# K and V caches of a decode step loaded through GpSimd's DMA queue, one packet for each DMA engine, instead of SP's

## The chip, the cores and the metric

The kernel runs on one core of one Trainium2 chip. The metric is the device time of one execution in microseconds, from the runs' times; the time before is the median of three. One further execution was recorded by the hardware profiler, and all rows come from it.

## The reference, cut to what matters

One decode step (one new token for each of two sequences) through a layer with attention and MLP in parallel, in float32:

```python
B, Sq, D = 2, 1, 1024;  Hq, Hkv, Sk, Dh = 32, 4, 32768, 128;  F = 3584
xn = _layernorm(x)
# attention over a cache, 8 query heads on each K/V head
q = (xn @ wq).reshape(B, 1, Hq, Dh)
scores = einsum(q, repeat(k_cache, 8)) * Dh ** -0.5
o = einsum(softmax(scores), repeat(v_cache, 8)) @ wo
# MLP
h = silu(xn @ w1)
return x + o + h @ w2
```

K and V are 134 MB each, the four weights 63 MB together. Every byte is read once, and there is little arithmetic on it.

## The kernel before, in words

There are three large buffers in SBUF, `bufA`, `bufB` and `bufC`, each of 128 partitions x 16384 float32 (64 KiB a partition, 8.39 MB). Everything that comes from HBM passes through them. The host has laid out every tensor so that a transfer is 128 rows, each row one contiguous run.

The order of the work is written out by hand, with semaphores between the engines, in three stages:

- **Weights at the head.** `blocks` (L152) lists four blocks of weights: `wq[0]` in `bufA`, `wq[1]` in `bufB`, the first 16384 columns of `w1` in `bufC`, and the remaining 12288 columns of `w1` (the `w1` tail, 6.29 MB) again in `bufB`. `first(u)` waits for the landing of block u and multiplies it with the normalised input; its last matmul's mark on TensorE's semaphore is `last_of[u]`. `second(u)` transposes the result. The first three blocks are loaded as soon as the program runs (`wq[1]` and `w1` after the 8 KB `x`, which ScalarE's queue loads, has landed, L115). The `w1` tail may be loaded once TensorE has read `wq[1]` out of `bufB`, that is after `last_of[1]` (L209).
- **Eight turns of attention.** There are 8 pairs of a K/V head and a sequence (`LOOPS`), and each turn takes four transfers of 8.39 MB: two halves of K into `bufA` and `bufB`, then two halves of V into the same two. `tick(it, k)` is TensorE's mark in turn `it`: 0 and 1 when it has read the K halves, 4 and 5 when it has read the V halves. A transfer into a buffer waits for the mark of the previous reader of that buffer. So there are at most two transfers on their way, one in each buffer. For the first turn the marks are `free = {0: last_of[0], 1: last_of[3]}`: `bufA` is free when `wq[0]` has been read, `bufB` when the `w1` tail has been read. TensorE runs the turns in a hardware loop (L291) and takes each landing off the semaphores `ldA` and `ldB` with `take` (a wait, then a decrement). Between the K and the V halves VectorE and ScalarE do the softmax.
- **Weights at the end.** `wo[0]` into `bufA` after `tick(7, 4)`, `wo[1]` into `bufC`, and `w2` in pieces into `bufB` after `tick(7, 5)` and into `bufA` after `wo[0]` has been read.

All large transfers, of weights and of K and V, are issued by SP through `load` (L204 to L207): wait for the mark, then issue. SP does this strictly in the order of the program text:

```python
    load(bufB[:, :(N1 - 4) * SUB], w1[:, W:], ldB, last_of[1])     # L209
    ...
    free = {0: last_of[0], 1: last_of[3]}
    for it in range(LOOPS):                                          # L231
        load(bufA, kt[b, h, 0], ldA, tick(it - 1, 4) if it else free[0])
        load(bufB, kt[b, h, 1], ldB, tick(it - 1, 5) if it else free[1])
        load(bufA, v[b, h, 0], ldA, tick(it, 0))
        load(bufB, v[b, h, 1], ldB, tick(it, 1))
```

GpSimd fills some constants at the head (L104 to L110) and has no work after that.

Of the kernel before, what the change touches and what calls it, by code (L numbers as in the profile page):

```python
# [18 lines left out]
LOOPS = HKV * B  # L19
# [35 lines left out]
def gqa_plus_mlp_kernel(nc, x, kt, v, wq, wo, w1, w2, out):  # L55


    pe, dve, act, pool = (Stream(nc, e, n) for e, n in
                          ((nc.tensor, "pe"), (nc.vector, "dve"), (nc.scalar, "act"), (nc.gpsimd, "pool")))
    sp = nc.sync  # L60
    sems = [pe.sem, dve.sem, act.sem, pool.sem]

    def sem(name):
        sems.append(nc.alloc_semaphore(name))
        return sems[-1]

    def sb(name, *shape):
        return nc.alloc_sbuf_tensor(name, shape, F32).ap()
# [3 lines left out]

    bufA, bufB, bufC = (sb(n, P, W) for n in ("bufA", "bufB", "bufC"))
    ldA, ldB, ldC, ldx, ldr, done = (sem(n) for n in ("ldA", "ldB", "ldC", "ldx", "ldr", "done"))
    tq, tps, trm, tgd, te, tls, tob = (sem(n) for n in ("tq", "tps", "trm", "tgd", "te", "tls", "tob"))
    ident, ones, sel, fold = sb("ident", P, P), sb("ones", P, P), sb("sel", P, 32), sb("fold", P, 64)
    st = sb("st", P, 2 * NC, 16, 32)
# [18 lines left out]
    def mm(o, lhsT, rhs, start=True, stop=True):  # L96
        return nc.tensor.matmul(o, lhsT, rhs, start=start, stop=stop)  # L97
# [5 lines left out]
    g = nc.gpsimd  # L103
# [100 lines left out]
    def load(buf, src, s, *ticks):  # L204
        for of, n in ticks:
            sp.wait_ge(of.sem, n)
        sp.dma_start(buf, src).then_inc(s, 16)  # L207
# [18 lines left out]
    def tick(it, k):  # L226
        return pe, start + PER * it + k + 1

    dve.eng.sem_inc(tps, NC)
    free = {0: last_of[0], 1: last_of[3]}  # L230
    for it in range(LOOPS):  # L231
        h, b = divmod(it, B)
        load(bufA, kt[b, h, 0], ldA, tick(it - 1, 4) if it else free[0])
        load(bufB, kt[b, h, 1], ldB, tick(it - 1, 5) if it else free[1])
        load(bufA, v[b, h, 0], ldA, tick(it, 0))
        load(bufB, v[b, h, 1], ldB, tick(it, 1))

    def queries(it):
        if it:
# [6 lines left out]
    for it in range(LOOPS):  # L246
        h, b = divmod(it, B)
# [43 lines left out]
    with nc.tensor.While(lambda: nc.tensor.snap(turn) < LOOPS):  # L291
        pe.take(tq)
        for a in range(4):
            buf = (bufA, bufB)[a // 2]
            if a % 2 == 0:
                pe.take((ldA, ldB)[a // 2], 16)
                pe.take(tps)
            for r in range(4):
                for q4 in range(4):
                    n = (4 * (a % 2) + q4) * 4 + r  # L300
                    m = mm(ps[a][32 * q4:32 * q4 + 32, :], qT[:, 32 * r:32 * r + 32], buf[:, n * 512:(n + 1) * 512],
                           r == 0, r == 3)
            if a % 2:
                pe.mark(m, LOOPS)
        pe.take(trm)
        pe.mark(mm(smA[:REP, :P], rm, ident), LOOPS)
        pe.take(tgd)
        pe.mark(mm(smB[:, :REP], ones[:REP, :], gd), LOOPS)
        for a in range(4):
            buf = (bufA, bufB)[a // 2]  # L310
            if a % 2 == 0:
                pe.take((ldA, ldB)[a // 2], 16)
                pe.take(te)
            for j in range(16):
                q4, n = j % 4, 16 * (a % 2) + j
                m = mm(po[32 * q4:32 * q4 + 32, :], st[:, a, j, :], buf[:, n * 512:(n + 1) * 512],
                       a == 0 and j < 4, a == 3 and j >= 12)
            if a % 2:
                pe.mark(m, LOOPS)
        pe.take(tls)  # L320
        pe.mark(mm(smA[:, :REP], ones, lsum), LOOPS)
        pe.take(tob)
        for r in range(4):
            m = mm(smB[:, :REP], ob[:, r * P:(r + 1) * P], sel[:, REP * r:REP * (r + 1)], r == 0, r == 3)
        pe.mark(m, LOOPS)
        nc.tensor.reg_add(turn, turn, 1)
# [6 lines left out]
    def stream(buf, src, cuts, *ticks):  # L333

        for lo, hi in zip(cuts, cuts[1:]):
            s = sem(f"piece{len(pieces)}")
            load(buf[:, lo:hi], src[:, lo:hi], s, *ticks)
            pieces.append((hi, s))
            yield hi, s

    lo = 11 * D
    plan = [
        (bufA, [*stream(bufA, wo[0], (0, W), tick(LOOPS - 1, 4))], 0),
        (bufC, [*stream(bufC, wo[1], (0, W))], 16),
        (bufB, [*stream(bufB, w2[:, :W], (0, 4 * D, W), tick(LOOPS - 1, 5))], 32),
    ]
    acc2 = ps[0]
# [35 lines left out]
    for (hi, landed), (bank, a, e) in zip(ends[4:], banks):  # L383
        pe.wait((landed, 16))
        for j in range(4):
            at = lo + 4 * a + j * (e - a)
            m = mm(bank[32 * j:32 * j + 32, :e - a], hT[:, FT - 1, :], bufA[:, at:at + e - a], False, True)
        act.wait(pe.mark(m))
        i_ot = act.mark(nc.scalar.copy(ot[:, a:e], bank[:, :e - a]))  # L389
    sp.wait_ge(act.sem, i_ot[1])  # L390
    sp.dma_start(out, ot[::8, :]).then_inc(done, 16)
    sp.wait_ge(done, 16)
# [33 lines left out]
```

## Time and profile before

| | |
|---|---|
| time, median of 3 runs | 773.39 us (773.29 to 773.48) |
| span of the profiled execution, first to last instruction | 772.1 us |
| what lies around the span (median less span) | 1.3 us |
| bytes read from HBM | 331.37 MB, 429 GB/s over the span |
| TensorE busy | 389.2 us, 50% of the span |
| VectorE / ScalarE / GpSimd busy | 120.7 / 27.4 / 3.0 us |
| SP's DMA queue (q1) | 99.4% of the 16 DMA engines' span |

In the rows, PE is TensorE, DVE VectorE, ACT ScalarE, POOL GpSimd and SP SyncE; SPq and ACTq are the queues on which those engines issue transfers. A row of a timeline has the start in us from the span's start, the duration in us, engine, line, operation, output<-input, the number of instructions, and in brackets the idle time before them with what ended it. An issue's own duration is only the issuing; "us to landing" in the list of DMA issues is from the issue to the landing. One matmul of the program text appears as two MATMUL records. The profiled execution has no run time of its own beside its span.

### The profile page before, as it was taken

To read this page: it belongs to the slowest core of one execution; us is meant where nothing else is said; L and a number is where in the kernel's file an instruction comes from. 1 tells how busy PE (TensorE), PEld (TensorE's weight loads), DVE (VectorE), ACT (ScalarE), POOL (GpSimd) and SP (SyncE) were. 2 spreads that over 40 slices of the span, in tenths; PEclk is the share of its full clock that TensorE was granted. 3 is DMA by queue.
4 is the path that set the end of the run, shared out by engine and by line. 5 is a ranking of instruction groups with operands and counts; after the bars stand their busy time and mean duration, and the time that the engine had idled before them with its cause. 6 is when DMAs were issued, how large, how long until landed. Compare 5 with 4: busy or idle time off the path is not lost. (4 is left out here: it accounts for less than half of the span.)

```text
span 772.1 us, 5932 instructions
## 1 busy us (share of the span) xinstructions
PE 389.2 (50%) x2752; PEld 124.1 (16%) x2752; DVE 120.7 (16%) x153; ACT 27.4 (4%) x34; POOL 3.0 (0%) x10
## 2 busy tenths in 40 slices
PE   1555554464555454544464545454544464545456
PEld 1111211121111111111121111111111121111112
DVE  2000013111311131113111311131113111311000
ACT  0000101000100000001000100000001000000000
POOL 1000000000000000000000000000000000000000
PEclk9966767767767767767767767767767767767778
DMA  9999999999999999999999999999999999999997
GB/s 384 435 432 435 435 435 435 435 435 435 435 435 432 431 431 435 435 435 435 431 435 435 435 431 435 435 435 435 435 435 435 435 435 435 435 435 435 409 435 317
DMA packets 6676, 331.51 MB, mean 429 GB/s; under 512 B 758, under 2 KB 902, under 8 KB 1292
## 3 DMA queue, kind: packets, MB, share of 16 engines
q1 hardware_dynamic: 6656, 331.37, 99.4%
q8 instruction: 7, 0.11, 0.1%
q10 hardware_dynamic: 12, 0.02, 0.0%
q14 instruction: 1, 0.01, 0.0%
HBM read 331.37 MB, written 0.02 MB: 429 GB/s over the span
## 5 line engine op out<-in xcount | busy, mean ns | idle before, releaser
L97 PE MATMUL po<-bufB,st 128*32 128x512 f32 x512 | 72.3, 728 | 81.9 <-PEq L52 81.9
L97 PE MATMUL ps<-bufB,qT 128*32 128x512 f32 x512 | 71.8, 724 | 82.4 <-PEq L52 82.4
L97 PE MATMUL ps<-bufA,qT 128*32 128x512 f32 x512 | 72.5, 730 | 51.3 <-PEq L52 51.3
L97 PE MATMUL po<-bufA,st 128*32 128x512 f32 x512 | 72.9, 733 | 40.5 <-PEq L52 40.5
L275 DVE TENSOR_REDUCE ls<-st 128x8 f32<-128x1024 f32 x16 | 31.7, 1984 | 231.5 <-PE po L97 231.5
L250 DVE STREAM_TRANSPOSE st<-ps 128x1024 f32<-128x1024 f32 x16 | 20.0, 1249 | 247.8 <-PE ps L97 247.8
L97 PEld LDWEIGHTS po<-bufB,st 128*32 128x32 f32 x512 | 20.0, 131 | 134.2 <-issue 134.2
L97 PEld LDWEIGHTS ps<-bufB,qT 128*32 128x32 f32 x512 | 19.8, 130 | 134.4 <-issue 134.4
L97 PEld LDWEIGHTS ps<-bufA,qT 128*32 128x32 f32 x512 | 20.1, 131 | 97.2 <-issue 97.2
L97 PEld LDWEIGHTS po<-bufA,st 128*32 128x32 f32 x512 | 19.9, 131 | 87.0 <-issue 87.0
L252 DVE TENSOR_REDUCE mx<-st 128x8 f32<-128x1024 f32 x16 | 31.7, 1980 | 0.6
L272 ACT ACTIVATE st<-st 128x1024 f32<-128x1024 f32 x16 | 16.9, 1056 | 356.7 <-DVE st L271 356.1
L97 PE MATMUL ps<-bufB,xnT 128*32 128x512 f32 x112 | 19.0, 763 | 14.1 <-PEq L52 14.1
L271 DVE TENSOR_TENSOR st<-st,gmax 128x1024 f32<-128x1024 f32 x16 | 18.9, 1221 | 0.3
L97 PE MATMUL smA<-ident,rm 128*8 128x128 f32 x16 | 3.4, 301 | 29.4 <-PEq L52 29.4
L97 PE MATMUL ps<-bufC,oT 128*32 128x512 f32 x64 | 9.6, 770 | 10.3 <-DMA bufC<-in_wo 10.3
L97 PE MATMUL ps<-bufC,xnT 128*32 128x512 f32 x64 | 9.8, 783 | 9.6 <-DMA bufC<-in_w 9.6
L97 PE MATMUL smA<-lsum,ones 128*128 128x8 f32 x16 | 3.5, 290 | 19.2 <-PEq L52 19.2
L280 ACT COPY ob<-po 128x512 f32<-128x512 f32 x8 | 4.7, 585 | 238.6 <-PE po L97 238.6
L97 PE MATMUL ps<-bufB,hT 128*32 128x512 f32 x64 | 8.6, 688 | 8.1 <-DMA bufB<-in_w 8.1
L97 PE MATMUL ps<-bufA,oT 128*32 128x512 f32 x64 | 9.1, 729 | 7.1 <-DMA bufA<-in_wo 7.1
L97 PE MATMUL smA<-ident,st 2*128 2x2 f32 x16 | 3.6, 349 | 16.5 <-DVE st L136 16.5
(70 smaller groups left out, 109.7 us busy)
## 6 DMA issues: line engine op xcount, KB each, us to landing
bufB<-in_w SPq DMA_DIRECT2D x2, 6144.0 KB, 37.2
bufA<-in_w SPq DMA_DIRECT2D x1, 3072.0 KB, 36.9
bufB<-in_w SPq DMA_DIRECT2D x1, 2048.0 KB, 34.9
bufA<-in_w SPq DMA_DIRECT2D x1, 1536.0 KB, 40.3
bufA<-in_w SPq DMA_DIRECT2D x2, 512.0 KB, 41.5
bufA<-in_w SPq DMA_DIRECT2D x1, 384.0 KB, 42.3
bufA<-in_kt SPq DMA_DIRECT2D x8, 29.3
bufB<-in_kt SPq DMA_DIRECT2D x8, 29.3
```

The costliest lines, as they stand in the source:

```text
L97: return nc.tensor.matmul(o, lhsT, rhs, start=start, stop=stop)
L250: t = dve.mark(V.transpose(st[:, 2 * c:2 * c + 2].rearrange("p a j m -> p (a j m)"), pair[c]))
L252: m = V.tensor_reduce(mx[:, c, :], st[:, 2 * c:2 * c + 2].rearrange("p a j (r m) -> p m (a j r)", r=4), AX.X, ALU.max)
L271: act.wait(dve.mark(V.tensor_sub(e8[c], e8[c], gmax.to_broadcast([P, 128, REP]))))
L272: nc.scalar.activation(e8[c], e8[c], AF.Exp, scale=SCALE).then_inc(te, 1)
L275: m = V.tensor_reduce(ls[:, c, :], e8[c].rearrange("p n m -> p m n"), AX.X, ALU.add)
L280: nc.scalar.copy(ob, po).then_inc(tob, 1)
```

## The change

The 32 transfers of K and V are issued by GpSimd, with the same waits, the same order and the same shape. Each is asked for as one packet for each DMA engine: 128 rows over 16 engines are eight descriptors (rows of 64 KiB) for each. They count on two new semaphores, `kvA` and `kvB`. SP waits for these in order and hands each landing on by adding 1 to `inA` or `inB`, which TensorE takes in place of `ldA` and `ldB`. When all K and V have landed, GpSimd resets the state of those two semaphores and marks its own; SP waits for that mark at the very end. The weights stay on SP: its program is now the four transfers at the head, the 31 hand-ons, `wo[0]` and `wo[1]`, the last hand-on, then `w2` and the output.

```diff
+    kvA, kvB, inA, inB = (sem(n) for n in ("kvA", "kvB", "inA", "inB"))
...
     free = {0: last_of[0], 1: last_of[3]}
+    landed = 0
+
+    def packed(buf, src, s, *ticks):
+
+        pool.wait(*ticks)
+        g.dma_start(buf, src, single_packet=True).then_inc(s, 16)
+
+    def passed_on(upto):
+
+        nonlocal landed
+        while landed < upto:
+            s, to = ((kvA, inA), (kvB, inB))[landed % 2]
+            sp.wait_ge(s, 16 * (landed // 2 + 1))
+            sp.sem_inc(to, 1)
+            landed += 1
+
     for it in range(LOOPS):
         h, b = divmod(it, B)
-        load(bufA, kt[b, h, 0], ldA, tick(it - 1, 4) if it else free[0])
-        load(bufB, kt[b, h, 1], ldB, tick(it - 1, 5) if it else free[1])
-        load(bufA, v[b, h, 0], ldA, tick(it, 0))
-        load(bufB, v[b, h, 1], ldB, tick(it, 1))
+        packed(bufA, kt[b, h, 0], kvA, tick(it - 1, 4) if it else free[0])
+        packed(bufB, kt[b, h, 1], kvB, tick(it - 1, 5) if it else free[1])
+        packed(bufA, v[b, h, 0], kvA, tick(it, 0))
+        packed(bufB, v[b, h, 1], kvB, tick(it, 1))
+    for s in (kvA, kvB):
+        g.wait_ge(s, 16 * 2 * LOOPS)
+    g.dma_reset(range(kvA.num, kvB.num + 1))
+    g.sem_inc(pool.sem, 1)
+    pool.n += 1
+    passed_on(4 * LOOPS - 1)
...
-                pe.take((ldA, ldB)[a // 2], 16)
+                pe.take((inA, inB)[a // 2])
...
         (bufC, [*stream(bufC, wo[1], (0, W))], 16),
+    ]
+    passed_on(4 * LOOPS)
+    plan += [
         (bufB, [*stream(bufB, w2[:, :W], (0, 4 * D, W), tick(LOOPS - 1, 5))], 32),
     ]
...
+    sp.wait_ge(pool.sem, pool.n)
     sp.wait_ge(act.sem, i_ot[1])
     sp.dma_start(out, ot[::8, :]).then_inc(done, 16)
```

More of the change, by code (lines that the diff above doesn't have):

```diff
@@ L311, in gqa_plus_mlp_kernel @@
             if a % 2 == 0:
-                pe.take((ldA, ldB)[a // 2], 16)
+                pe.take((inA, inB)[a // 2])
                 pe.take(te)
```

## The prediction

> **What bounds the kernel now.** I read the page's 40 slices first, then its DMA queues, then SP's waits, and then SP's and TensorE's timelines around the two places where K/V transfers meet weight transfers.
>
> ```profile
> span 772.1 us, 5932 instructions
> DMA  9999999999999999999999999999999999999997
> GB/s 384 435 432 435 435 435 435 435 435 435 435 435 432 431 431 435 435 435 435 431 435 435 435 431 435 435 435 435 435 435 435 435 435 435 435 435 435 409 435 317
> q1 hardware_dynamic: 6656, 331.37, 99.4%
> q8 instruction: 7, 0.11, 0.1%
> SPq L207 <- PE ps L97: 394.2, 19, 38.3
> ```
>
> The DMA engines are busy from end to end, at 431 to 435 GB/s in all slices but the first, the last and one near the end. The last row is SP's own wait list: SP is idle most of the time, waiting until TensorE has read a buffer. So neither issuing nor computing is the limit: the bytes are, and the time changes only by what changes the rate or leaves the DMA engines with nothing to do. The span is 772.1 us, the median of the runs 773.39: 1.3 us lie around the span, and I carry them over.
>
> The steady state, in SP's timeline (start, duration, ...) and the list of issues (last number: us from issue to landing):
>
> ```profile
> 106.61 0.33 SPq L207 DMA_DIRECT2D bufA<-in_v  x1
> 144.76 0.33 SPq L207 DMA_DIRECT2D bufA<-in_kt  x1
> 667.11 0.33 SPq L207 DMA_DIRECT2D bufB<-in_v  x1
> 687.02 0.33 SPq L207 DMA_DIRECT2D bufA<-in_wo  x1
> bufA<-in_kt SPq DMA_DIRECT2D x8, 29.3
> bufB<-in_v SPq DMA_DIRECT2D x8, 29.3
> ```
>
> From 144.76 to 687.02 lie 28 transfers: 542.26 / 28 = 19.37 us each, for 8.389 MB: 433 GB/s. Issue to landing is 29.3 us, so each transfer is issued 29.3 - 19.37 = 9.9 us before the DMA engines get to it. That cover of 9.9 us is what the change draws on.
>
> **The change, part by part.**
>
> *1. The issue moves to GpSimd.* In the steady state a GpSimd issue may be later than SP's by anything up to 9.9 us at no cost. GpSimd has nothing else to do after the head, and its queue holds the same waits in the same order as SP's did. The trace has no issue by GpSimd. For SP's very first issue, onto idle DMA engines:
>
> ```profile
> 0.73 0.38 SPq L100 DMA_DIRECT2D bufA<-in_wq  x1
> 1.83 0.95 POOL L110 MEMSET oT<- 128x1024 f32 x1
> ```
>
> The first slice moves 384 GB/s and not 435: over 772.1 / 40 = 19.3 us that is 2.26 us lost, of which 0.73 precede the issue. So 1.53 us pass between an issue by SP and full speed. For GpSimd I add 0.7 us of work on the descriptors: bounded below by 0 (it is as quick as SP) and above by some 2 us (two of its longest operations here, the 0.95 us MEMSET). I take a value nearer to the MEMSET than to 0, because I expect GpSimd to write descriptors by program. Total 2.2 us, 1.5 to 3.5. The Trainium skill, "DMA: Bandwidth & Descriptors", section "Latency and other measured facts", gives 1 us to the first byte for GpSimd's path and 0.6 us for SP's; by these 0.4 us stand in place of my 0.7, and the sum below would be 0.3 us less. No run here shows it yet.
>
> *2. One packet instead of eight.* What this can bring is bounded by the rate: 8.389 MB at the best slice's 435 GB/s is 19.28 us against 19.37; 0.08 us x 31 = 2.6 us at most. On the other side, a gap between one GpSimd transfer and the next would cost 31 times its size. I take 0 for both: the slices at 431 and 435 lie within 1% and look alike at any place, so there is hardly a per-packet cost to take away.
>
> *3. SP hands on.* One wait and one increment for each landing, some tenths of a us (SP's whole issue takes 0.33). It lies between landing and matmul, so it comes off the same 9.9 us: 0. `wo[0]` stands behind the 31st hand-on, `w2` behind the 32nd; both landings precede the marks that those loads wait for anyway: 0. The reset at GpSimd's end runs beside the last 60 us of weights: 0.
>
> *4. The first K transfer leaves its place in SP's queue.* This is the part that counts. SP, ScalarE's queue, TensorE and VectorE at the head:
>
> ```profile
> 12.76 0.33 SPq L116 DMA_DIRECT2D bufB<-in_wq  x1
> 13.13 0.44 SPq L117 DMA_DIRECT2D bufC<-in_w  x1
> 51.92 0.33 SPq L207 DMA_DIRECT2D bufB<-in_w  x1
> 52.29 0.44 SPq L207 DMA_DIRECT2D bufA<-in_kt  x1
> 86.59 0.33 SPq L207 DMA_DIRECT2D bufB<-in_kt  x1
> ...
> 3.60 0.54 ACTq L112 DMA_DIRECT2D st<-in_x  x1
> ...
> 22.87 9.15 PE L97 MATMUL ps<-bufA,xnT 128*32 128x512 f32 x64 [2.82 <-PEq L52]
> 42.08 9.78 PE L97 MATMUL ps<-bufB,xnT 128*32 128x512 f32 x64 [10.06 <-PEq L52]
> 62.47 9.83 PE L97 MATMUL ps<-bufC,xnT 128*32 128x512 f32 x64 [9.62 <-DMA bufC<-in_w]
> 77.33 9.22 PE L97 MATMUL ps<-bufB,xnT 128*32 128x512 f32 x48 [4.05 <-PEq L52]
> 96.85 9.70 PE L97 MATMUL ps<-bufA,qT 128*32 128x512 f32 x64 [8.42 <-PEq L52]
> ...
> 89.86 0.17 DVE L242 COPY qT<-qall 128x32 f32<-128x32 f32 x1
> ```
>
> `bufA` is free when `wq[0]` has been read, at 22.87 + 9.15 = 32.02. But SP issues the first K half at 52.29 only, because the `w1` tail stands ahead of it in the queue and waits for `last_of[1]` (42.08 + 9.78 = 51.86). So the DMA engines get `wq[1]`, `w1`, `w1` tail, first K half. That order does a service: the tail lands at 77.3, TensorE reads it until 86.55, SP issues the second K half into the same `bufB` at 86.59, and all that time the first K half (19.4 us, landed at 96.85) keeps the DMA engines busy.
>
> In the changed kernel GpSimd waits for `last_of[0]` alone and issues the first K half at about 32. Then two queues have work. How they share is seen in `x`: 8 KB on ScalarE's queue, issued at 3.60 into the middle of `wq[0]`, had landed when SP, which waits for it, went on at 12.76, while `wq[0]` was still being moved (TensorE starts on it at 22.87). So the DMA engines take turns between queues, after a piece and not after a whole transfer. The Trainium skill says the same (same page, section "Queues, rings and completion order"): each DMA engine goes round the queues and changes only at the end of a packet. By that rule the first K half, one packet for each engine, is moved in one go once its turn comes; by turns of single rows it would share half and half with the weights. The sum is the same under both: by about 81 it is done, before the tail gets its share.
>
> So the order becomes: `wq[1]`'s first part, first K half, rest of `wq[1]`, `w1`, `w1` tail. The bytes up to that point are those of before, so they end where they ended, at about 96.8, but now the `w1` tail is the last of them (`wq[1]` lands some 19.4 us later, at 61.4; TensorE has read it at 71.2, so the tail is still queued well before `w1` ends at 81.8). At 96.8 the DMA engines have nothing: the second K half waits for the tail to be read, the first V half for the first K half, and TensorE turns to that only after the four blocks. From the tail's landing:
> - TensorE reads the tail: from 77.33 to SP's issue at 86.59, 9.26 us; 0.1 us for the landing's signal;
> - GpSimd's issue to full speed: 2.2 us.
>
> The sum is 11.6 us in which nothing moves. It isn't made up later, since the bytes are the limit. What is late next: TensorE starts on the first K half 3.6 us after the tail (89.86 + 0.17 less 86.55, the transposes, SiLU and `qT`), needs 9.7 us, and the first V half is issued some 13.3 us after the tail was read, while the second K half still has 19.4 - (13.3 - 2.2) = 8 us to go: covered, and the steady state goes on as before.
>
> *5. The end.* `wo[0]` is issued at 687.02 when the last V half has about 9.4 us to go. If that is one packet, nothing changes. If it shares row by row, it lands 9.4 us later, and `w2` is issued that much later; but `wo[0]` and `wo[1]`, 2 x 19.3 us, are queued behind: 0.
>
> Forecast: 773.4 + 11.6 = 785.0 us. Its own bounds: 773.4 + 9.4 + 1.5 - 2.6 = 781.7 below, 773.4 + 9.4 + 3.5 = 786.3 above.
>
> **The rivals.**
>
> *A. No hole: the K half doesn't get past the weights.* If the DMA engines serve SP's queue first while it has work, or if the first GpSimd issue comes late enough to be moved beside the tail, the first K half covers the tail's reading as now. Then only part 2 remains: 773.4, or down to 770.8 if one packet brings the full 2.6 us. Against it: `x` got through beside `wq[0]` within 9 us, and 30 us lie between the mark at 32 and the tail's turn. For it: `x` went through ScalarE's queue and not GpSimd's. 10%: 5% faster by over 0.2% (1.5 us, about what a measurement of this kernel can tell from no change), 5% within it.
>
> *B. The hole, and a gap at each transfer.* If the next GpSimd transfer's descriptors are not taken up while the last one is running, each of 31 transfers pays part of a cold start. At a quarter of the 1.53 us: 0.4 x 31 = 12 us, 797; at the whole of it, 47 us, 832. Against it: descriptors can lie ready 9 us ahead. For it: no GpSimd transfer is in the trace. 15% for gaps up to 0.4 us, 5% for more. The Trainium skill (same page, "Measured") has 425 GB/s for large transfers issued by GpSimd; taken as the steady rate, a transfer would be 19.74 us by an estimate from that page, and the time some 11 us above my forecast, inside this case.
>
> *C. Instruction fetches.* The 7 packets of q8 are fetches of code. Beside rows they wait for a row of about 2.4 us (19.37 / 8), beside one packet for up to 19.4 us. Only a fetch that an engine needs at once costs this, and TensorE idles before nearly every block; one exposed fetch would give up to 785 + 9.5 (19.4 less the cover), 795. 3%.
>
> **How the numbers follow.** The forecast has 67%, A 10%, B 20%, C 3%. The range takes in the forecast's own bounds, B's small gaps and C, and leaves out A and the large gaps (15%): 781.0 to 797.0. Faster 0.05, within 0.2% 0.05, slower 0.90.
>
> **What would show it.** In the profile after: an issue of the first K half by GpSimd at about 32; TensorE's start on `wq[1]` at about 61 and not 42; the `w1` tail's matmuls near 97; one slice about 97 to 108 with the DMA share halved, and all later marks 11 to 12 us later; the spacing of transfers still 19.3 to 19.4 us. If TensorE starts on `wq[1]` at 42 and no slice drops, A was right. If the spacing is 19.6 or more, B.

## The result, and the profile after

The changed kernel takes 787.47 us (median of 4 runs, 787.16 to 787.75) against 773.40: 1.0182 times as long, 95% interval 1.0167 to 1.0196. The profiled execution has a span of 786.4 us, 14.3 more. First the page of the changed kernel: the span, the DMA share and the rate in 40 slices, and the two queues.

```profile
span 786.4 us, 5967 instructions
DMA  9999759999999999999999999999999999999997
GB/s 407 447 424 427 324 213 431 457 437 430 427 430 430 427 430 460 433 427 430 430 430 427 453 440 430 427 430 433 427 427 460 433 430 427 430 433 427 428 437 311
q0 software_dynamic: 4608, 268.44, 78.9%
q1 hardware_dynamic: 2048, 62.93, 18.7%
```

The loss has one place: slices 5 and 6, from 78.6 to 118 us, where the DMA share falls to 7 and 5 tenths. Everywhere else the digits are those of before. GpSimd's and SP's issues there (first two fences: start, duration, and the idle time before with what ended it), and TensorE's work:

```profile
32.29 0.67 POOL L237 DMA_DIRECT2D bufA<-in_kt  x1 [28.72 <-PE ps L98]
106.77 0.53 POOL L237 DMA_DIRECT2D bufB<-in_kt  x1 [73.82 <-PE ps L98]
120.49 0.53 POOL L237 DMA_DIRECT2D bufA<-in_v  x1 [13.19 <-PE ps L98]
158.90 0.53 POOL L237 DMA_DIRECT2D bufA<-in_kt  x1 [19.39 <-PE po L98]
681.29 0.53 POOL L237 DMA_DIRECT2D bufB<-in_v  x1 [17.68 <-PE ps L98]
```

```profile
58.99 0.33 SPq L208 DMA_DIRECT2D bufB<-in_w  x1
700.93 0.33 SPq L208 DMA_DIRECT2D bufA<-in_wo  x1
```

```profile
22.68 9.28 PE L98 MATMUL ps<-bufA,xnT 128*32 128x512 f32 x64 [5.03 <-PEq L52]
49.33 9.60 PE L98 MATMUL ps<-bufB,xnT 128*32 128x512 f32 x64 [17.38 <-PEq L52]
81.91 8.68 PE L98 MATMUL ps<-bufC,xnT 128*32 128x512 f32 x64 [21.99 <-DMA bufC<-in_w]
96.59 9.86 PE L98 MATMUL ps<-bufB,xnT 128*32 128x512 f32 x48 [5.02 <-PEq L52]
110.38 9.79 PE L98 MATMUL ps<-bufA,qT 128*32 128x512 f32 x64 [2.05 <-PEq L52]
130.29 8.38 PE L98 MATMUL ps<-bufB,qT 128*32 128x512 f32 x64 [10.12 <-PEq L52]
```

The first K half is issued at 32.29. The `w1` tail is read from 96.59 and not from 77.33, and the second K half issued at 106.77 and not at 86.59. From there all is late by the same amount: the last V half by 681.29 - 667.11 = 14.2 us, the first `wo` by 700.93 - 687.02 = 13.9. The spacing is (681.29 - 158.90) / 27 = 19.35 us a transfer, the same as before. The hole in a window of its own (columns: window, its length, busy time of PE, PEld, DVE, ACT and POOL, the granted clock, the DMA share, GB/s):

```profile
82.00:96.60 14.60, 9.58 (x74) 3.02 (x75) 0.26 (x2) 0.58 (x1) 0.00 (x0) 0.85 0.78 338
96.60:110.00 13.40, 11.73 (x64) 4.40 (x64) 1.38 (x6) 2.11 (x3) 0.53 (x1) 0.75 0.22 78
110.00:130.00 20.00, 9.79 (x64) 2.64 (x64) 3.23 (x2) 0.00 (x0) 0.53 (x1) 0.67 0.97 420
```

The view counts a row whole in the window in which it starts. So the 78 GB/s of the window from 96.6 to 110 are the first 16 rows of the second K half alone (16 x 65536 bytes in 13.4 us), and they start at 108.0 to 108.6: while TensorE reads the tail, nothing moves. The engines are idle even before it starts. By the trace's records of single rows, cut at the window's ends, they are busy for 87% of the 14.6 us up to 96.6 (the view's 0.78 leaves out what is left at 82 of rows begun before), so 1.9 us are lost there. 14 of the 16 DMA engines end their last row of the tail between 94.2 and 94.8, the two slowest at 96.0 and 96.1, and the landing is the slowest one's. On the mean an engine is idle from 94.66 to 108.25, 13.6 us, and its first row takes 3.0 us and not 2.4: 14.2 us together, the whole of the loss.

Why are two engines slower? The records don't name the engine, but a row starts where the record before it on its engine ends, within 0.05 us, so the rows can be strung together. The two late engines are the two that had an instruction fetch between their rows, a packet of 16 KiB on queue q8. The one at 58.21 took 0.95 us and the row after it 2.92 us in place of 2.42, and that engine stayed some 1.4 us behind the others until the tail's end. The one at 92.74 took 0.97 us, and the last row after it 2.32 us in place of 1.81. 14 engines had marked the landing by 95.15, these two at 96.38 and 96.45. So by the trace 1.3 us of the hole come from two instruction fetches. The traces of e2, e3, e4 and e6 below show the same: two fetches up to then, and two late engines. No run takes the fetches away, so this rests on the traces alone.

### The profile page after: what moved, and what is told of

The parts are those of the page before. It is cut to its first block, busy times and chain, and to the rows that moved or that the text cites. A ratio compares the mean times of both kernels' runs of the same rounds, so it can differ in the third digit from the quotient of the medians.

```text
span 786.4 us, 5967 instructions
## 1 busy us (share of the span) xinstructions
PE 401.6 (51%) x2752; PEld 128.7 (16%) x2752; DVE 120.7 (15%) x153; ACT 27.4 (3%) x34; POOL 20.0 (3%) x42
## 5 line engine op out<-in xcount | busy, mean ns | idle before, releaser
L98 PE MATMUL po<-bufB,st 128*32 128x512 f32 x512 | 75.7, 757 | 87.3 <-PEq L52 87.3
L98 PE MATMUL ps<-bufB,qT 128*32 128x512 f32 x512 | 73.7, 740 | 80.8 <-PEq L52 80.8
L98 PE MATMUL ps<-bufA,qT 128*32 128x512 f32 x512 | 74.6, 748 | 41.5 <-PEq L52 41.5
L98 PE MATMUL po<-bufA,st 128*32 128x512 f32 x512 | 74.8, 750 | 38.2 <-PEq L52 38.2
L98 PE MATMUL smB<-sel,ob 128*128 128x8 f32 x64 | 12.9, 331 | 0.0
L98 PEld LDWEIGHTS smB<-sel,ob 128*128 128x128 f32 x64 | 12.6, 291 | 0.0
```

## The experiments

Theory T: the loss is the order of the transfers in the DMA engines; the first K half gets ahead of the `w1` tail, and nothing covers the reading of the tail. Rival G: GpSimd's path is slower, at the start or at each transfer. The packet setting is a rival of its own. Ratios are to the kernel before, timed on the same chip.

**The first K half after `w1` has been read (e1).**

```diff
-    free = {0: last_of[0], 1: last_of[3]}
+    free = {0: last_of[2], 1: last_of[3]}
```

> The changed kernel with one mark changed: GpSimd issues the first K half when TensorE has read the third block (w1) and not when it has read wq[0], so at about 72 us, when only the w1 tail is left on SP's queue (it ends at about 77). Theory T (order): the tail is nearly done, the first K half follows it and covers TensorE's reading of the tail; no hole, 773.4 to 775.5 us. Rival G (GpSimd's path is slow at the start or at each transfer): still 785 or more. Rival in between: the K half's first rows push the tail's last one or two rows back by 2 to 5 us, but the K half still covers the reading, so this costs nothing either.

Measured: 774.22 us, ratio 1.0009 (0.9999 to 1.0019). All 32 transfers are on GpSimd's queue, and the hole is gone. GpSimd's and TensorE's timelines of e1, and its rates:

```profile
71.63 0.67 POOL L237 DMA_DIRECT2D bufA<-in_kt  x1 [68.06 <-PE ps L98]
88.85 0.53 POOL L237 DMA_DIRECT2D bufB<-in_kt  x1 [16.55 <-PE ps L98]
...
80.01 8.51 PE L98 MATMUL ps<-bufB,xnT 128*32 128x512 f32 x48 [7.75 <-PEq L52]
97.12 8.49 PE L98 MATMUL ps<-bufA,qT 128*32 128x512 f32 x64 [6.72 <-PEq L52]
GB/s 381 434 435 435 434 435 434 435 434 431 434 434 435 431 434 434 434 431 431 434 434 434 434 434 434 434 434 431 434 434 434 434 434 434 434 434 434 411 433 317
```

The tail is read from 80.0, 2.7 us later than before, and K from 97.1, where it was before the change. By the records no row of K stands between the tail's own rows, which end by 77.0. 14 engines mark the landing by 76.1. On the two slowest, a row of K comes before the mark, and they mark it at 79.5 and 79.9. T holds; G would have needed 785.

**The same, after `wq[1]` has been read (e2).** `free = {0: last_of[1], ...}`: the issue is then at SP's old time.

> The changed kernel with one mark changed: GpSimd issues the first K half after wq[1] has been read (about 52 us, the very time at which SP issued it before). Theory T (order in the DMA engines, not the time of issue): the rows of the K half take turns with w1's last rows and with the tail's, so K is done at about 91 and the tail last, at about 96; the hole stays, 786 to 788 us. Rival (what counts is only that K was issued 20 us too early): 773.4 to 776.

Measured: 787.93 us, 1.0185 (1.0168 to 1.0202). GpSimd's timeline of e2, then TensorE's:

```profile
52.41 0.67 POOL L237 DMA_DIRECT2D bufA<-in_kt  x1 [48.83 <-PE ps L98]
106.97 0.53 POOL L237 DMA_DIRECT2D bufB<-in_kt  x1 [53.89 <-PE ps L98]
...
70.08 9.56 PE L98 MATMUL ps<-bufC,xnT 128*32 128x512 f32 x64 [17.03 <-DMA bufC<-in_w]
96.78 9.86 PE L98 MATMUL ps<-bufB,xnT 128*32 128x512 f32 x48 [16.14 <-PEq L52]
```

Before the change SP issued the same transfer at 52.29, so the time of issue isn't it. On a queue of its own it takes turns with the rest of `w1` (read from 70.1 and not 62.5) and with the tail, which is last again, at 96.8.

**No GpSimd transfer at all (e3).** The kernel before, with SP issuing the first K half ahead of the tail:

```diff
+    load(bufA, kt[0, 0, 0], ldA, last_of[0])
     load(bufB[:, :(N1 - 4) * SUB], w1[:, W:], ldB, last_of[1])
...
-        load(bufA, kt[b, h, 0], ldA, tick(it - 1, 4) if it else free[0])
+        if it:
+            load(bufA, kt[b, h, 0], ldA, tick(it - 1, 4))
```

> The kernel before, all transfers on SP, nothing on GpSimd; only the first K half is issued ahead of the w1 tail in SP's program. Theory T: the tail is the last of the bytes again, and the second K half waits for its reading: a hole of about 10 us of reading and signals, 2 us between most DMA engines' end and the slowest one's, and 1.5 us of start: 786 to 788 us without any GpSimd transfer. Rival G: without GpSimd no loss, 773.4 to 775. If GpSimd's start is worth 0.7 us more than SP's, this kernel is 0.7 us below the changed one.

Measured: 786.95 us, 1.0175 (1.0158 to 1.0192). SP's timeline of e3, then TensorE's:

```profile
31.58 0.33 SPq L207 DMA_DIRECT2D bufA<-in_kt  x1
106.17 0.33 SPq L207 DMA_DIRECT2D bufB<-in_kt  x1
...
96.70 9.42 PE L97 MATMUL ps<-bufB,xnT 128*32 128x512 f32 x48 [23.64 <-PEq L52]
129.48 5.83 PE L97 MATMUL ps<-bufB,qT 128*32 128x512 f32 x40 [9.84 <-PEq L52]
```

The order by itself, on SP's queue alone, costs 13.5 us of the 14.1. What GpSimd adds is small: the runs are 0.5 us apart (787.47 and 786.95). In the traces it is, from the end of the reading to its issue 0.3 us (96.59 + 9.86 = 106.45, 106.77) against 0.05 for SP, and from issue to TensorE's start 23.5 us (130.29 - 106.77) against 23.3 (129.48 - 106.17). The first rows start 1.48 us after GpSimd's issue on the mean, and 1.24 after SP's.

**Without the request for one packet (e4, e11).** `single_packet=True` is left out: in the changed kernel (e4), and in e1, where there is no hole (e11).

> The changed kernel without the request for one packet for each engine. In the changed kernel's trace rows of K and of wq[1] alternate on each DMA engine although one packet was asked for. Theory T: the packet setting changes nothing that matters: 787.5 within 0.5 us, TensorE's start on wq[1] at about 49 again. Rival (one packet does help or hurt at each transfer): off by up to 2.6 us either way, and a different start on wq[1].

> The e1 kernel (first K half issued after w1 has been read, so no hole) without the request for one packet: the packet setting by itself where nothing else is lost. If it changes nothing, 774.2 within 0.7 us. If one packet brings part of the 2.6 us that the prediction left open, this is 1 us or more slower than e1; if it costs e1 its 0.8 us, this is at 773.4.

Measured: e4 787.15 us, 1.0175 (1.0158 to 1.0192); e11 774.12 us, 1.0008 (0.9999 to 1.0017). In e4 TensorE starts on `wq[1]` where it did with the request:

```profile
49.32 9.75 PE L98 MATMUL ps<-bufB,xnT 128*32 128x512 f32 x64 [17.21 <-PEq L52]
```

The request changes nothing that could be measured, neither the rate nor the turns. With it as without it, `wq[1]` is late by 7.2 us, three rows of 2.42 us, and not by the 19.4 of a whole transfer. In the records of the changed kernel a row of GpSimd's queue and a row of SP's take turns on every engine from 36.2 us on. Two rows of K come between rows of `wq[1]`, and a third between its last row (done by 46.4) and the marks of its landing (48.6 to 49.2).

**One transfer put back (e5).** SP issues the first K half in its old place; 31 transfers stay on GpSimd. The counts that SP and GpSimd wait for are changed to fit and left out here.

```diff
...
-        packed(bufA, kt[b, h, 0], kvA, tick(it - 1, 4) if it else free[0])
+        if it:
+            packed(bufA, kt[b, h, 0], kvA, tick(it - 1, 4))
+        else:
+            load(bufA, kt[b, h, 0], ldA, free[0])
...
```

> The changed kernel with one transfer put back: the first K half is issued by SP in its old place behind the w1 tail; the other 31 transfers of K and V stay on GpSimd, one packet asked for, landings handed on by SP. Theory T (the whole loss is the place of the first K half): 773.2 to 774.5 us, the hole gone. Rival G (part of the loss is GpSimd's path): 1 us or more above 773.4.

Measured: 775.20 us, 1.0017 (1.0007 to 1.0027), in two groups: four runs at 773.5 to 773.8, six at 775.1 to 775.5. The profiled run is one of the first group (773.51). Its TensorE and GpSimd timelines:

```profile
101.55 9.24 PE L98 MATMUL ps<-bufA,qT 128*32 128x512 f32 x64 [13.05 <-PEq L52]
116.26 8.72 PE L98 MATMUL ps<-bufB,qT 128*32 128x512 f32 x64 [5.47 <-PEq L52]
...
86.94 0.67 POOL L237 DMA_DIRECT2D bufB<-in_kt  x1 [83.38 <-PE ps L98]
111.13 0.53 POOL L237 DMA_DIRECT2D bufA<-in_v  x1 [23.51 <-PE ps L98]
```

The hole is gone, but T's 774.5 was missed by six of ten runs, and the median, 1.75 us above the kernel before, meets the sign set for G (1 us or more). G as a cost of each GpSimd transfer doesn't fit the other four runs, nor e1, which has all 32 transfers on GpSimd's queue and is 0.8 us above. What costs the six runs 1.7 us is open. One difference is seen in the trace: the two K halves are now on two queues and take turns, so the first is read from 101.55 and not 96.85, and the first V half is issued 5.1 us before TensorE starts on the second K half, where before it was 116.25 - 106.61 = 9.6. That is near the edge of the cover that e8 to e10 measure below, which would fit the second group of 1.7 us; no run of that group was profiled, so this isn't shown.

**The tail read twice (e6 in the changed kernel, e7 in e1).** The 24 matmuls of the fourth block are done twice:

```diff
-        for k in range(KT):
+        for again in range(2 if u == 3 else 1):
+            for k in range(KT):
```

> The changed kernel in which TensorE reads the w1 tail twice (its 24 matmuls are repeated, each pass starting the sum anew). Theory T: the reading lies wholly in the hole, so the time grows by the whole second reading: 9.2 to 9.9 us, to 796.5 to 797.5. Rival (the hole has another cause, the reading is beside it): about 787.5.

> The same doubled reading of the tail, but in the kernel in which GpSimd issues the first K half after w1 has been read (e1, 774.2 us; the tail is read from 80.0, TensorE starts on K at 97.1). Theory T: the first K half covers most of it. The second K half is issued at about 98.2 instead of 88.9. If the cover ends when K's landing is seen (97), the loss is 98.2 + 1.5 - 97, some 3 us: 777. If an issue onto idle DMA engines takes 23.5 us to land, 4 us more than 19.4, as in the changed kernel's trace, it lands at 121.7 and not at 116.5: 5 us, 779. Rival (reading costs the same anywhere): 783.5 or more.

Measured: e6 793.72 us, 1.0261 (1.0244 to 1.0279); e7 776.90 us, 1.0044 (1.0026 to 1.0061). TensorE and GpSimd in e6, then in e7:

```profile
96.88 15.59 PE L98 MATMUL ps<-bufB,xnT 128*32 128x512 f32 x96 [4.55 <-PEq L52]
112.80 0.53 POOL L238 DMA_DIRECT2D bufB<-in_kt  x1 [79.06 <-PE ps L98]
```

```profile
95.67 0.53 POOL L238 DMA_DIRECT2D bufB<-in_kt  x1 [23.23 <-PE ps L98]
119.40 9.31 PE L98 MATMUL ps<-bufB,qT 128*32 128x512 f32 x64 [11.36 <-PEq L52]
```

A second pass takes 5.7 us (15.59 - 9.86) and not the 9.2 expected, so e6 is some 3 us below what was expected, and e7's 776.90 agrees with its 777 by luck: that reckoning, done again with the issue at 95.67, gives 95.67 + 1.5 - 97, next to no loss. The other one, by an issue's 23.5 us to landing, gives 95.67 + 23.5 = 119.2 against 116.5, the 2.7 us measured. What the two runs were to tell apart stands: in the hole the issue is 6.0 us later (112.80, 106.77) and the kernel 6.3; in e1 the same work moves the issue by 6.8 us (95.67, 88.85) and costs 2.7. An issue at 95.67, before the first K half's landing is seen, already costs something.

**The cover measured (e8, e9, e10).** In e1, GpSimd fills a buffer that nobody reads any more, 12, 21 or 6 times, between the wait and the issue, in turns 2 to 8:

```diff
         pool.wait(*ticks)
+        if it:
+            for _ in range(12):
+                pool.wait(pool.mark(g.memset(pr[0], 0.0)))
         g.dma_start(buf, src, single_packet=True).then_inc(s, 16)
```

> The e1 kernel in which GpSimd, between the wait and the issue, makes 12 memsets of 128x512 of a buffer that nobody reads any more (some 7 us), ahead of each transfer of turns 2 to 8 (28 of them). It measures the cover on which part 1 of the prediction rests. By the prediction's 9.9 us: all covered, 774 to 775 us. By the other reading, that a late issue takes 23.5 us to land and a buffer's round is 9.5 (reading) + 0.3 + 7 + 23.5 = 40.3 us against two transfers' 38.7: 1.6 us for each of 14 pairs, 794 to 797.

> As the one before with 21 memsets (some 12.5 us). By the prediction's 9.9 us of cover: 2.6 to 2.9 us more for each pair or each transfer, 810 to 855 us. By the round of 9.5 + 0.3 + 12.5 + 23.5 = 45.8 us against 38.7: 7.1 us for each of 14 pairs, 870 to 876.

> As the two delayed kernels (e1 with memsets by GpSimd between the wait and the issue, in turns 2 to 8), with 6 memsets, some 3.6 us. It looks for the point where the cover ends: 7.2 us of delay cost 31 us (2.2 for each of 14 pairs), 12.5 us cost 83 (5.9 for each pair). A straight line through these reaches zero at 4.1 us. If the cover is a sharp edge near there, 774 to 775.5 us; if the loss sets in gradually (each DMA engine has its own lag), 776 to 785.

GpSimd's timelines give the delays: e10, e8 and e9, the fills and the issue after them.

```profile
301.43 3.43 POOL L239 MEMSET pr<- 128x512 f32 x6 [13.96 <-PE po L98]
305.16 0.53 POOL L240 DMA_DIRECT2D bufA<-in_kt  x1 [0.30 <-POOL pr L239]
```

```profile
306.40 6.92 POOL L239 MEMSET pr<- 128x512 f32 x12 [12.58 <-PE po L98]
313.62 0.53 POOL L240 DMA_DIRECT2D bufA<-in_kt  x1 [0.30 <-POOL pr L239]
355.19 0.54 POOL L240 DMA_DIRECT2D bufA<-in_v  x1 [0.71 <-POOL pr L239]
```

```profile
324.05 12.16 POOL L239 MEMSET pr<- 128x512 f32 x21 [10.83 <-PE po L98]
336.51 0.53 POOL L240 DMA_DIRECT2D bufA<-in_kt  x1 [0.30 <-POOL pr L239]
381.20 0.54 POOL L240 DMA_DIRECT2D bufA<-in_v  x1 [0.71 <-POOL pr L239]
```

| delay of each issue | time, us | ratio | above e1, per pair of transfers |
|---|---|---|---|
| 3.7 us (e10) | 774.37 | 1.0009 (1.0000 to 1.0019) | 0.0 us |
| 7.2 us (e8) | 805.24 | 1.0413 (1.0396 to 1.0431) | 2.2 us |
| 12.5 us (e9) | 856.99 | 1.1067 (1.1026 to 1.1107) | 5.9 us |

3.7 us cost nothing that the medians show (the runs of e10 reach from 773.4 to 776.6, and the profiled one is the slowest), 7.2 us cost 31 us in all. So the cover is not 9.9 us: it ends between 3.7 and 7.2, and the line through the two later points meets zero at 4.1. The later the issue, the shorter is the way to the landing: at the median 29.0 us in e1, 25.4 in e10, 24.5 in e8 and 22.3 in e9. So the way gives back 3.6, 4.5 and 6.7 us of the three delays, and what is left, 0.1, 2.7 and 5.8, is near the loss for each pair.

Both expectations in us were missed. One round of a buffer in e9 is 381.20 - 336.51 = 44.7 us (45.8 expected), and on the mean of turns 2 to 8 it is 44.6, so 870 to 876 was too high by 13 us or more. In e8 one round is 355.19 - 313.62 = 41.6 us and the mean 40.8 (40.3 expected), and 794 to 797 was too low by 8 us or more. The 0.5 us that a round is longer than reckoned make up 7 of them over 14 pairs; where they come from was not tried.

## Why the prediction was right, point by point

The direction, the place and the mechanism were as forecast, and 787.47 lies within the range. 785.0 was 2.5 us too low.

- *Part 4, the order.* Right. e3 makes the loss without GpSimd, and e1 and e5 take the hole away with GpSimd. The time of issue was not what counts (e2).
- *Part 4, the sum, 11.6 us forecast and 14.1 measured.* The most mis-sized term is the landing's 0.1 us. The DMA engines don't end together: from their mean end at 94.66 to TensorE's start at 96.59 lie 1.9 us, which the prediction, putting their end at 96.8, left out. 1.3 of these are the two engines with an instruction fetch. The reading and the signals were 10.2 us (96.59 to 106.77) and not 9.26: TensorE took 9.86 for the tail, and GpSimd 0.3 to issue.
- *Part 1, the start.* 2.2 us forecast; the issue to the first rows' start is 1.5 us on the mean, and those rows take 0.6 longer: 2.1. But it is not GpSimd's price: SP pays nearly the same (e3, 23.3 against 23.5 us to TensorE's start). The added 0.7 us should have been some 0.2 (1.48 less 1.24). The 0.4 us that the prediction worked out from the Trainium skill ("DMA: Bandwidth & Descriptors", section "Latency and other measured facts") was nearer.
- *Part 1, the cover of 9.9 us.* Wrong, without harm here: GpSimd needed a few tenths of it. The error was to take issue to landing less 19.4 us as the time that an issue may be late. A late issue takes 22 to 25 us to land and not 19.4, as the hole, e8 and e9 show; e10 and e8 put the true cover between 3.7 and 7.2 us.
- *Part 2, the packet.* 0 was right (e4, e11), and so was the spacing (19.35 us). The turns were left open between packets and single rows; they were rows. By the Trainium skill ("DMA: Bandwidth & Descriptors", section "Queues, rings and completion order") a DMA engine changes queues at the end of a packet; here it did so after each 64 KiB row of 2.42 us, whether one packet was asked for or not. If the request made one packet at all can't be seen in the trace. TensorE's start on `wq[1]`, forecast at 61 by the packet rule, came at 49.3 for this reason; the sum is the same under both, as the prediction had it. The first K half's last row ends at 71.7, before the tail's turn.
- *What is late next, in part 4.* 89.86 + 0.17 - 86.55 is 3.5 and not 3.6; nothing hangs on it. The first V half was issued 14.0 us after the reading (120.49 - 106.45; 13.3 forecast), and was covered.
- *Parts 3 and 5.* Nothing is lost there: the loss is 14.2 us at the last V half and 14.3 at the end of the span. The rows took turns at the end too: `w2` was issued at 727.90 and not 705.24, 22.7 us later, so 8.7 beyond the loss, as part 5 said for turns of rows.
- *The rivals.* A fell with the hole; e1 is the kernel that A described. B fell with the spacing. The page of the Trainium skill cited there ("DMA: Bandwidth & Descriptors", section "Measured", 425 GB/s) doesn't describe this case: the steady rate of GpSimd's transfers is 8.389 MB / 19.35 us, 433 GB/s, SP's own. C, at 3%, named fetches only as something that an engine waits for. The traces show another way in which they cost: two fetches each put a DMA engine behind, and the landing with it, by 1.3 us. In the kernel before the same two fetches cost nothing: 14 engines mark the tail's landing by 75.8 and two at 77.0 and 77.2, but the first K half is already queued behind.

No version beat the kernel before. e1 and e11 come to within 0.1% of it.

## What to carry to other kernels

A queue that issues strictly in order also decides which transfer lies between two others. When one is moved to another queue, look for the transfer that it used to stand behind, and for the reading that it used to cover: here a single K transfer out of 32 made the whole difference, and one index in its wait gave it back. The time by which an issue may be late is not the issue-to-landing time less the transfer's own: landing is the slowest DMA engine's, and a start on idle engines has its price, so measure it by delaying the issue.

## What the runs showed of the hardware that was not expected

GpSimd's transfers of 8.39 MB ran at SP's rate (19.35 us each), and their first rows started 1.48 us after the issue, SP's 1.24. Rows of 64 KiB from two queues took turns one by one, with one packet asked for too, and a row of the other queue could come between a transfer's last row and the mark of its landing (in the changed kernel for `wq[1]`, in e1 for the tail). An instruction fetch of 16 KiB took 0.95 us between the rows of one DMA engine and put it some 1.4 us behind the others. An 8.39 MB transfer issued onto idle DMA engines took 23.2 us to land, 4 more than its steady share of 19.35.
